# Attention with two experts per token: the second attention product with the probabilities as stationary operand

## The chip, the cores and the metric

The kernel runs on one core of one Trainium2 chip. The metric is the device time of one execution in microseconds (us). A core has five engines with a queue of instructions each: TensorE (PE; the loading of its stationary operand is shown apart, as PEld), VectorE (DVE), ScalarE (ACT), GpSimd (POOL) and SyncE (SP, which issues most DMAs). Each engine works through its queue in order and waits at semaphores for the others.

## The reference

```python
# attention: q, k, v are [4, 8, 768, 64]; each row sees 4 sink keys and the last 128 keys
scores = np.matmul(q, k.transpose(0, 1, 3, 2)) / np.sqrt(D)
scores = np.where(is_sink | in_window, scores, -1e9)
a = np.exp(scores - scores.max(-1, keepdims=True))
a = a / (a.sum(-1, keepdims=True) + 1e-9)
x = np.matmul(a, v)                                  # -> [3072 tokens, 512]
# experts: 8 of them, two for each token
noisy = x @ w_gate + np.log1p(np.exp(x @ w_noise)) * noise
top2 = the two largest of noisy; top2_w = softmax over these two
out[t] = sum over both: top2_w * (np.maximum(x[t] @ w1[e], 0) @ w2[e])
```

## The kernel before

The program is written as a list of operations with a planner. Each `op(engine, cost, priority, function, r=, w=, u=)` names its engine, a cost in us that the author gave it, a priority and what it reads and writes; `Plan.run` plays the list through and so fixes the order of the instructions on each engine. The priorities are place numbers plus the offsets of the table `PR`. `plan.rings` gives the number of buffers of each name; an operation on buffer n waits for all work on buffer n minus that number.

There are two phases. Phase one is the attention of four batches, each of four pairs of heads (`HP`), each pair in three steps (`NJ`) of 256 rows: 48 steps, called n below. One step holds four blocks u: two row blocks j of 128 rows times two heads h. Behind every fourth pair the routing of that batch is mixed in (logits, top two, where each token goes). Phase two has the logits and the routing of the last batch and then the experts, in which PE multiplies without a break. Expert 0 begins on tokens of the first three batches while the last batch is routed.

A step runs like this, with the names in the profile:

- `turn` (tile T, L283): PE transposes keys and queries of the step; ACT copies them to `kq`.
- `qk` (tile S, L310): the scores, as two matmuls that use 64 of PE's 128 rows each, side by side. ACT (`prev`, L313) and DVE (`cur`, L318/L320) put the window together in `cbuf`, 132 numbers for a row: four sink keys and 128 keys of the window.
- `mins` (L330): DVE takes the maximum of each row; POOL subtracts it (L197); ACT takes the exponential (L337).
- `sums` (L340) and `sums_i` (L348): DVE adds up each row of `cbuf` and takes the reciprocal, kept in `ri` for the whole batch.
- `ptr` (tile P, L368): PE transposes the four blocks of probabilities; ACT copies them to `CT`; `ptr_m` (CM, L378 on DVE or L380 on POOL) makes the copy with the part above the diagonal. The row of a key in the window is either in this block of keys or the one ahead, so the second product is `CT` times the values `vn` of the block ahead plus `CM` times the difference `dv` of the two blocks.
- `pv` (tile X, L394 and L397): the second product with the values as stationary operand, 64 columns wide, and the transposed probabilities moving, 128 columns. The heads of a pair go to the two halves of PE's columns and run side by side. The result is transposed: 64 dimensions by 128 rows.
- `pctr` (L385), `sink_c`, `sinks` (L406): the four sink keys, from a packed tile `pcbuf`, turned by PE, copied by ACT to `ps`, then two matmuls with `vr` (sink values) stationary.
- `pv_c` (L414): ACT copies the transposed result to `xtn`. `rows` (L419): PE transposes it back to rows; `rows_c` (L422): DVE multiplies by `ri`, and SP stores the rows (`xr`) to the table `x_rows` in HBM.
- `logits` (lines 605 to 645, twelve times: three per batch): `proj` (L616) multiplies the not yet normalised `xtn` with `wbd`, in which each head has its own columns, four matmuls side by side in four strips of 32 columns; ACT copies, PE turns (`turn`, L624), DVE scales each head by `ri` (L627) and adds the heads up (L632).

In the trace a float32 matmul has two records, since PE goes through its data twice, with a load of the stationary operand ahead of each; a float32r matmul and a transpose have one.

Of the kernel before, what the change touches and what calls it, by code (L numbers as in the profile page):

```python
# [9 lines left out]
F32 = mybir.dt.float32  # L10
# [7 lines left out]
OP = mybir.AluOpType  # L18
AX = mybir.AxisListType
BIG = 1.0e30  # L20
PR = dict(dv_pool=2, cm_pool=10, gap=3, pc_pool=0, warm=1, cur=-28.393, cur1=3.934, cur1_0=-210.795, cur1_9=-0.214,
          cur_0=-6.435, cur_9=42.546, dv=-181.673, dv_0=-58.475, dv_9=-165.981, exps=924.339, exps_0=-284.526,
          exps_9=-135.434, ga=442.815, gt=5.527, ksink=329.474, ksink_9=351.649, lg=5.452, load_qk=4.916, load_v=-10.311,
          mins=-1.124, mins_0=-130.078, mins_9=-231.976, nosink=115.551, nosink_0=201.297, nosink_9=23.605,
          pcopy=-1100.148, pcopy_0=54.064, pcopy_9=13.8, plow=6.687, plow_0=155.036, plow_9=-170.043, prev=-313.725,
          prev_0=560.262, prev_9=8.445, ptr=-158.634, ptr_0=-7.014, ptr_9=481.977, ptr_c=113.881, ptr_c_0=180.788,
          ptr_c_9=110.108, ptr_m=-225.012, ptr_m_0=-135.409, ptr_m_9=-137.504, pv=-1.694, pv_0=1.459, pv_9=2.578,
          pv_c=-36.493, pv_c_0=-19.005, pv_c_9=0.119, qk=-419.785, qk_0=3.807, qk_9=316.006, rows=-857.853,
          rows_0=-458.314, rows_9=34.438, rows_c=-1553.261, rows_c_0=-208.37, rows_c_9=-15.709, rt=-558.501, sink_c=2.596,
          sink_c_0=-90.91, sink_c_9=-279.362, sinks=-714.907, sinks_0=-12.828, sinks_9=261.99, sub=318.235, sub_0=521.605,  # L30
          sub_9=182.999, sums=78.667, sums_0=135.936, sums_9=-1.546, sums_i=-160.405, sums_i_0=280.185, sums_i_9=-301.562,
          t0=11.199, t2=-37.957, tgroup=71.501, tgroup_0=-63.73, tgroup_9=-56.402, tgroup_c=-1595.788, tgroup_c_0=7.035,
          tgroup_c_9=-3.093, w1=579.923, ksink_0=-652.007, stay=3844.16, pctr_0=71.802, sinkv=185.095, sc_dve=2,
          pctr=-325.901, pctr_9=-655.681)
# [165 lines left out]
def attention(tc, plan, consts, cst, sh, q, k, v, xbuf):  # L200
# [4 lines left out]
    KW = 128 + NS  # L205
    NP = sh.B * HP
    plan.rings.update(vr=2, kn=2, qn=2, vn=2, dv=2, skn=2, sqn=2, kq=2, C=5, mn=3, sm=4, ri=2, pc=3,
                      CT=2, CM=2, ps=3, xr=3, S=2, P=1, T=1, X=2, xtn=5, lt=1, lm=1, lg=2)
# [8 lines left out]
    m1 = consts.tile([128, NS], F32, name="m1")  # L217
    nc.vector.tensor_copy(m1, m0[:, :NS])
    nc.vector.memset(m0[:, :NS], 0.0)

    cbuf = consts.tile([128, plan.rings["C"], 4, KW + 1], F32, name="cbuf")
    nc.gpsimd.memset(cbuf[:, :, :, KW:], 1e-9)

    pcbuf = consts.tile([128, plan.rings["pc"], 128], F32R, name="pcbuf")
    nc.gpsimd.memset(pcbuf.bitcast(F32), 0.0)
    bit = [consts.tile([128, 1], dt, name=nm) for nm, dt in (("biti", I32), ("bit", F32))]
# [6 lines left out]
    def C(n):  # L233
        return cbuf[:, n % plan.rings["C"], :, :KW]
# [18 lines left out]
    def sink_hi(b):  # L253
        nc.scalar.activation(get("vr", b, [128, 2, HP, 2, D], F32R), vs(b), AF.Copy)

    def sink_lo(b):

        t = get("vr", b)
        nc.vector.scalar_tensor_tensor(t, t.bitcast(F32), bit, vs(b), op0=OP.mult, op1=OP.add)
# [10 lines left out]
    def load_v(g):  # L270
        nc.sync.dma_start(get("vn", g, [128, 2, NB, D]),
                          dram(v, g * 2 * S * D, [[D, 128], [S * D, 2], [128 * D, NB], [1, D]]))

    def dv(g, eng):
        x = get("vn", g)
# [49 lines left out]
    def cur1(n):  # L325
        c = C(n)[:, 2:, NS:2 * NS]
        nc.vector.tensor_tensor(c, c, m1[:, None, :].to_broadcast([128, 2, NS]), op=OP.add)
# [10 lines left out]

    def sums(n):
# [1049 lines left out]
```

## Time and profile before

| | before |
|---|---|
| median of 3 runs | 805.64 us (805.34 to 808.08) |
| profiled execution, from the first to the last instruction (span) | 802.8 us |
| left around the span, against the median | 2.8 us |
| PE busy | 772.3 us, 96% |
| DVE busy | 434.3 us, 54% |
| POOL busy | 441.5 us, 55% |
| ACT busy | 342.6 us, 43% |
| mean granted PE clock | 0.993 |

No time of the profiled execution other than its span is given, so the 2.8 us beside it are the median less the span. Busy time on PE counts a matmul from its start to its modelled end, and matmuls overlap: a new one may start every 0.11 us while each is counted as 0.27 us. So a busy PE is read from how closely the starts follow each other, and the share of busy time only says that there are few breaks. In the rows of the trace "128*64 128x128" says that the stationary operand is 128 rows by 64 columns and that the result is 128x128 in size as the program counts it (128 moving columns for L394), and xN is the count of records.

### The profile page before, as it was taken

How to read it: one execution, taken by the hardware profiler on the slowest of the kernel's cores; microseconds unless marked ns; L12 is line 12 of the kernel's file. 1: busy time of each engine (PE TensorE's matmuls, PEld its weight loads, DVE VectorE, ACT ScalarE, POOL GpSimd, SP SyncE). 2: the span in 40 equal slices, each digit the busy share in tenths (PEclk: the TensorE clock that was granted, in tenths of full speed). 3: DMA queues.
4: the chain of work that ended last, by engine and by line, in shares of the span. 5: the costliest groups of instructions: out<-in, count | busy, mean ns of one | idle time of the engine just before them, and what ended most of it. 6: DMA issues, size and time to landing. Idle time of an engine off the chain costs nothing.

```text
span 802.8 us, 13806 instructions
## 1 busy us (share of the span) xinstructions
PE 772.3 (96%) x4753; PEld 656.1 (82%) x4753; DVE 434.3 (54%) x1115; ACT 342.6 (43%) x695; POOL 441.5 (55%) x669
## 2 busy tenths in 40 slices
PE   7999999899798999999999999999999999999996
PEld 4776777677577888988988898899889999999994
DVE  5888897798565345354435434542553363364320
ACT  5877778686420334244233413332442343334121
POOL 5757657778604447473745456374636647366222
PEclk9999999999999999999999999999999999999998
DMA  6769767845526196264526535561744365174133
GB/s 121 169 150 200 162 155 207 181 120 129 152 90 175 22 257 152 45 140 128 102 38 158 141 56 94 144 119 37 147 123 94 73 172 121 26 175 97 32 40 40
DMA packets 151193, 96.03 MB, mean 120 GB/s; under 512 B 100528, under 2 KB 129200, under 8 KB 151120
## 3 DMA queue, kind: packets, MB, share of 16 engines
q1 hardware_dynamic: 137744, 67.93, 32.6%
q0 software_dynamic: 13376, 27.19, 19.4%
q8 instruction: 38, 0.62, 0.3%
q14 instruction: 35, 0.29, 0.1%
HBM read 66.89 MB, written 28.20 MB: 118 GB/s over the span
## 4 chain that ended last, share of the span: by engine, by line
PE 64%; issue 4%; DMA 2%; POOL 2%; DVE 1%; SPq 0%; ACT 0%; POOLq 0%; DVEq 0%; ACTq 0%
PE H L1070 11%; PE H L1072 10%; PE H L1071 10%; PE Y L1099 10%; PE Y L1101 10%; PE Y L1100 10%; POOL out L1123 1%; PE Y L1104 1%; PE Y L1105 1%; DMA xg<-x_rows,idg 1%; DMA out<-y,idx 1%; DMA st<-in_moe_w 1%; SPq L1268 0%; PE T L947 0%; PE X L616 0%
## 5 line engine op out<-in xcount | busy, mean ns | idle before, releaser
L903 POOL DMA_INDIRECT xg<-x_rows,rt_idq x174 | 175.8, 1010 | 62.1 <-issue 51.7
L1070 PE MATMUL H<-skn,w 128*128 128x384 f32 (+4 forms) x512 | 178.3, 348 | 0.0
L1072 PE MATMUL H<-skn,w 128*128 128x384 f32 (+4 forms) x512 | 176.8, 345 | 0.0
L1071 PE MATMUL H<-sqn,w 128*128 128x384 f32 (+4 forms) x512 | 176.3, 344 | 0.0
L1088 DVE SCALAR_TENSOR_TENSOR h<-H,h 128x384 fp32r<-128x384 f32 (+4 forms) x168 | 75.5, 469 | 184.7 <-ACT h L1081 184.5
L1081 ACT ACTIVATE h<-H 128x384 fp32r<-128x384 f32 (+4 forms) x128 | 64.6, 505 | 249.4 <-PE H L1072 249.3
L1132 POOL COPY spacer<-h 1x1 f32<-1x1 f32 x88 | 26.6, 303 | 167.3 <-ACT h L1081 167.1
L1123 POOL DMA_INDIRECT out<-y,idx x53 | 89.2, 1683 | 50.4 <-ACT y L1108 34.6
L1070 PEld LDWEIGHTS H<-skn,w 128*128 128x128 f32 x512 | 96.6, 189 | 7.7 <-issue 0.8
L1071 PEld LDWEIGHTS H<-sqn,w 128*128 128x128 f32 x512 | 96.6, 189 | 6.9
L1072 PEld LDWEIGHTS H<-skn,w 128*128 128x128 f32 x512 | 96.4, 188 | 3.0
L1101 PE MATMUL Y<-w2b,h 128*128 128x512 f32 x192 | 75.2, 392 | 1.1 <-DVE h L1088 1.1
L1099 PE MATMUL Y<-w2b,h 128*128 128x512 f32 x192 | 75.5, 393 | 0.6 <-ACT h L1081 0.6
L1099 PE MATMUL Y<-w2a,h 128*128 128x512 f32 x192 | 75.5, 393 | 0.0
L1100 PE MATMUL Y<-w2b,h 128*128 128x512 f32 x192 | 75.2, 392 | 0.0
L1100 PE MATMUL Y<-w2a,h 128*128 128x512 f32 x192 | 75.1, 391 | 0.0
L1101 PE MATMUL Y<-w2a,h 128*128 128x512 f32 x192 | 74.9, 390 | 0.0
L197 POOL TENSOR_TENSOR cbuf<-cbuf,mn 128x528 f32<-128x528 f32 x48 | 52.6, 1098 | 18.5 <-DVE mn L330 10.7
L310 PE MATMUL S<-kq 64*128 64x264 f32 (+1 forms) x384 | 56.4, 410 | 1.0 <-DVE ri L348 0.5
L961 ACT ACTIVATE skn<-xtn 128x512 fp32r<-128x512 f32 (+2 forms) x46 | 27.9, 606 | 63.3 <-DVE xtn L952 63.2
L197 DVE TENSOR_TENSOR w<-st,w 128x1024 fp32r<-128x1024 f32 x28 | 34.3, 1224 | 17.8 <-ACT w L1008 17.8
L1101 PEld LDWEIGHTS Y<-w2b,h 128*128 128x128 f32 x192 | 36.1, 188 | 9.4 <-DVE h L1088 1.6
(209 smaller groups left out, 1359.6 us busy)
## 6 DMA issues: line engine op xcount, KB each, us to landing
st<-in_moe_w SPq DMA_DIRECT2D x36, 512.0 KB
st<-in_moe_w SPq DMA_DIRECT2D x112, 128.0 KB
out<-zt SPq DMA_DIRECT2D x31, 256.0 KB
vn<-in_v SPq DMA_DIRECT2D x16, 384.0 KB
x_rows<-xr SPq DMA_DIRECT2D x48, 128.0 KB
kn<-in_k SPq DMA_DIRECT2D x30, 192.0 KB
qn<-in_q SPq DMA_DIRECT2D x30, 192.0 KB
xg<-x_rows,rt_idq POOLq DMA_INDIRECT x174, 2.9
```

What stands on the lines that cost most here:

```text
L197: eng.tensor_tensor(out, a, b, op=OP.subtract)
L310: nc.tensor.matmul(p[:, :2 if j else 1], kq(g)[r, j // 2, 2 + j % 2, NS:], x[:, :2 if j else 1], start=True, stop=True)
L903: nc.gpsimd.indirect_dma_start(out=x[:, i, :], out_offset=None, in_=xbuf.rearrange("r (q d) -> (r q) d", d=sh.SW), in_offset=bass.Indirect ...
L1070: nc.tensor.matmul(p, w[:, 0, i], xh, start=(i == 0), stop=False)
L1071: nc.tensor.matmul(p, w[:, 0, i], xl, start=False, stop=False)
L1072: nc.tensor.matmul(p, w[:, 1, i], xh, start=False, stop=(i == DC - 1))
L1081: nc.scalar.activation(get("h", FC * q + f, [128, 2 * 128 * FIRST], F32R)[:, :width], get("H", FC * q + f), AF.Relu)
L1088: nc.vector.scalar_tensor_tensor(h[:, o:o + s1 - s0], p[:, s0:s1], 0.0, h[:, s0:s1].bitcast(F32), op0=OP.max, op1=OP.subtract)
L1099: nc.tensor.matmul(p, hh, w[:, 0], start=(f == 0), stop=False)
L1100: nc.tensor.matmul(p, hh, w[:, 1], start=False, stop=False)
L1101: nc.tensor.matmul(p, hl, w[:, 0], start=False, stop=(f == FC - 1))
L1123: d = nc.gpsimd.indirect_dma_start(out=out, out_offset=bass.IndirectOffsetOnAxis(ap=c["idx"][:size(e, t), e, t:t + 1], axis=0), in_=get("y ...
```

## The change

`pv` has its operands exchanged: the transposed probabilities `CT` and `CM` (128 by 128) are stationary, and the values move: 65 columns, of which the last one is all ones, so that the row sum comes out of the same product (64 for `dv`). The result stands in rows. Four blocks of 66 columns (`DV`) stand beside each other in tile X. The sinks are one matmul with `ps` stationary and 264 moving columns, with a column of ones for each block (`units`, `counts`) and 1e-9 added through row 64 of `pcbuf`. `sums` and `sums_i` go; `ri` is the reciprocal of the sum columns in PSUM, and `rows_c` normalises before the transposes. `rows` then transposes the normalised rows and ACT copies them to `xtn` (`rows_t`). The logits are taken from that: 128 tokens of `xtn` stationary, `wgn` (16 columns) moving, eight matmuls that add up in PSUM, and one copy. The two loads `wgn` replace four of `wbd`. `cur1` goes from DVE to POOL. The table `PR` is new: with `dv_pool` 0 all sixteen `dv` are on DVE, of which eight were on POOL, and with `cm_pool` 7 (was 10) of 12 twelve more `ptr_m` are on DVE.

```diff
+    DV = D + 2
-                      CT=2, CM=2, ps=3, xr=3, S=2, P=1, T=1, X=2, xtn=5, lt=1, lm=1, lg=2)
+                      CT=2, CM=2, ps=3, xr=3, S=2, P=1, T=1, X=2, xtn=5, lg=2)
...
+    vnbuf = consts.tile([128, plan.rings["vn"], 2, NB, DV], F32, name="vnbuf")
+    nc.gpsimd.memset(vnbuf[:, :, :, :, D:], 1.0)
+    vrbuf = consts.tile([128, plan.rings["vr"], 2, HP, 2, DV], F32R, name="vrbuf")
...
-        nc.vector.tensor_tensor(c, c, m1[:, None, :].to_broadcast([128, 2, NS]), op=OP.add)
+        nc.gpsimd.affine_select(c, c, pattern=[[0, 2], [-1, NS]], base=0, channel_multiplier=1, compare_op=OP.is_ge, fill=-BIG)
...
-    def sums(n):
-        nc.vector.tensor_reduce(get("sm", n, [128, 4]), cbuf[:, n % plan.rings["C"]], op=OP.add, axis=AX.X)
...
     def pv(n):
...
-                    nc.tensor.matmul(o, get("vn", g)[:, h, max(j - 1, 0), :], get("CT", n)[:, u, :], start=(u < 2),
-                                     stop=False, skip_group_check=True)
+                    nc.tensor.matmul(o[:, :D + 1], get("CT", n)[:, u, :], vn(g)[:, h, max(j - 1, 0), :D + 1], start=(u == 0),
+                                     stop=False, skip_group_check=True)
...
-                    nc.tensor.matmul(o, get("dv", g)[:, h, j - 1, :], get("CM", n)[:, u, :], start=False, stop=False,
+                    nc.tensor.matmul(o[:, :D], get("CM", n)[:, u, :], get("dv", g)[:, h, j - 1, :], start=False, stop=False,
...
-        for a in range(2):
-            nc.tensor.matmul(get("X", XA[n])[:, a, :], get("vr", b)[:, a, i].rearrange("p h d -> p (h d)"), get("ps", n),
-                             start=False, stop=True, skip_group_check=True)
+        nc.tensor.matmul(get("X", XA[n])[:, :4 * DV], get("ps", n), vr(b)[:, :, i].rearrange("p a h d -> p a (h d)"),
+                         start=False, stop=True, skip_group_check=True)
+
+    def ri(n):
+        nc.vector.reciprocal(get("ri", n, [128, 4]), out(n)[:, :, D])
+
+    def rows_c(n):
+        nc.vector.tensor_tensor(get("xr", n, [128, 4, D], F32, "tail"), out(n)[:, :, :D],
+                                get("ri", n)[:, :, None].to_broadcast([128, 4, D]), op=OP.mult)
+
     def rows(n):
...
+            nc.tensor.transpose(x[:, c * 128:(c + 1) * 128], get("xr", n)[:, 2 * c:2 * c + 2].rearrange("p h d -> p (h d)"), idf)
...
-            op("PE", .95 if jj else .7, n + .6 + P(g, "pv"), lambda n=n: pv(n),
-               r=[("vn", g), ("CT", n), ("dv", g), ("CM", n), ("X", xa)], w=[("X2", xa)], kind=2)
+            op("PE", .92 if jj else .7, n + .6 + P(g, "pv"), lambda n=n: pv(n),
+               r=[("vn", g), ("CT", n), ("dv", g), ("CM", n), ("X", xa)], w=[("X2", xa)])
...
     def proj():
-        p = get("X", xa, [128, 4, 128], F32, "ps")
-        for i, g in enumerate(pairs):
-            nc.tensor.matmul(p[32 * i:32 * (i + 1), :2, :], c["wbd"][:, i].rearrange("p h a e -> p (h a e)"),
-                             get("xtn", g)[:, jj * 256:(jj + 1) * 256], start=True, stop=True)
+        p = get("X", xa, [128, 512], F32, "ps")
+        for t in range(2):
+            for i, g in enumerate(pairs):
+                nc.tensor.matmul(p[:, 2 * E * t:2 * E * (t + 1)], get("xtn", g)[:, (2 * jj + t) * 128:(2 * jj + t + 1) * 128],
+                                 c["wgn"][:, i].rearrange("p a e -> p (a e)"), start=(i == 0), stop=(i == HP - 1))
...
-    def turn():
-    def scale():
-    def total():
```

Where the first logits of the first batch stand, PE's queue had before (T: keys and queries turned, S: scores, P: probabilities turned, `lt`: the logits to be turned):

```order
L616 MATMUL X<-xtn,wbd 32x256 x4
L385 MATMUL X<-idf,pcbuf 128x128
L283 MATMUL T<-idf,kn 128x128 x2
L283 MATMUL T<-idf,qn 128x128 x2
L310 MATMUL S<-kq 128x264 x4
L394 MATMUL X<-CT,vn 64x128 x4
L397 MATMUL X<-CM,dv 64x128 x4
L406 MATMUL X<-ps,vr 128x128 x2
L310 MATMUL S<-kq 128x264 x4
L419 MATMUL X<-idf,xtn 128x128 x2
L368 MATMUL P<-idf,cbuf 128x128 x4
L624 MATMUL X<-idf,lt 128x128 x2
```

The same place in PE's queue has now:

```order
L406 MATMUL X<-vnbuf,CT 128x65 x4
L409 MATMUL X<-dv,CM 128x64 x4
L623 MATMUL X<-wgn,xtn 128x16 x8
L304 MATMUL T<-idf,kn 128x128 x2
L304 MATMUL T<-idf,qn 128x128 x2
L378 MATMUL P<-idf,cbuf 128x128 x4
L417 MATMUL X<-vrbuf,ps 128x264
L331 MATMUL S<-kq 128x132 x2
L331 MATMUL S<-kq 128x264 x2
L430 MATMUL X<-idf,xr 128x128 x2
```

The second product keeps its eight matmuls, now with 128 result rows and 65 or 64 moving columns; the logits go from four to eight matmuls and lose their transposes; the sinks go from two to one. The transposes of the rows (L430) stand behind the scores, and read `xr`, which DVE writes.

On DVE a stretch with the rows of two steps read before (mn: the maxima, sm: the sums, xr: the normalised rows):

```order
L340 TENSOR_REDUCE sm_722<-cbuf_146 128x4
L330 TENSOR_REDUCE mn_734<-cbuf_146 128x4
L348 RECIPROCAL ri_264<-sm_722 128x2x2
L320 COPY_PREDICATED cbuf_146<-le_137,S_736 128x2x128
L422 TENSOR_TENSOR xr_759<-X_637,ri_264 128x256
L422 TENSOR_TENSOR xr_767<-X_639,ri_264 128x256
L320 COPY_PREDICATED cbuf_146<-le_137,S_748 128x2x128
```

and a stretch of that kind reads now:

```order
L351 TENSOR_REDUCE mn_601<-cbuf_143 128x4
L421 RECIPROCAL ri_637<-X_575 128x4
L421 RECIPROCAL ri_639<-X_578 128x4
L424 TENSOR_TENSOR xr_642<-X_575,ri_637 128x256
L424 TENSOR_TENSOR xr_649<-X_578,ri_639 128x256
L341 COPY_PREDICATED cbuf_143<-le_136,S_634 128x2x128
L341 COPY_PREDICATED cbuf_143<-le_136,S_651 128x2x128
```

The reduction for the sums is gone, the reciprocals read tile X, so that they stand behind the sinks of PE, and PE's transposes of the rows stand behind `xr`, where before they stood behind ACT's copy and `xr` came last.

More of the change, by code (lines that the diff above doesn't have):

```diff
@@ L20 @@
 BIG = 1.0e30
[L21 to L34, printed above, removed]
@@ L205, in attention @@
     KW = 128 + NS
+    DV = D + 2
     NP = sh.B * HP
-    plan.rings.update(vr=2, kn=2, qn=2, vn=2, dv=2, skn=2, sqn=2, kq=2, C=5, mn=3, sm=4, ri=2, pc=3,
-                      CT=2, CM=2, ps=3, xr=3, S=2, P=1, T=1, X=2, xtn=5, lt=1, lm=1, lg=2)
+    plan.rings.update(vr=2, kn=2, qn=2, vn=2, dv=2, skn=2, sqn=2, kq=2, C=5, mn=3, ri=3, pc=3,
+                      CT=2, CM=2, ps=3, xr=3, S=2, P=1, T=1, X=2, xtn=5, lg=2)
     get, op = plan.get, plan.op
@@ L233, in C, with vn, vr, counts @@
     def C(n):
-        return cbuf[:, n % plan.rings["C"], :, :KW]
+        return cbuf[:, n % plan.rings["C"]]
+    def vn(g):
+        return vnbuf[:, g % plan.rings["vn"]]
+    def vr(b):
+        return vrbuf[:, b % plan.rings["vr"]]
+    def counts():
+        for r in range(plan.rings["vr"]):
+            for a in range(2):
+                nc.vector.tensor_copy(vrbuf[:, r, a, :, :, D:], units[:, None, 2 * a:2 * a + 2, :].to_broadcast([128, HP, 2, 2]))
     def vs(b):
@@ L381, in ptr_m, with out @@
                                     compare_op=OP.is_ge, fill=0.0)
+    def out(n):
+        return get("X", XA[n])[:, :4 * DV].rearrange("p (u d) -> p u d", d=DV)
     def pctr(n):
-        x = get("X", XA[n], [128, 4, 128], F32, "ps")
-        nc.tensor.transpose(x[:, 2, :], pcbuf[:, n % plan.rings["pc"], :].bitcast(F32), idf)
+        x = get("X", XA[n], [128, 512], F32, "ps")
+        nc.tensor.transpose(x[:, 4 * DV:4 * DV + 128], pcbuf[:, n % plan.rings["pc"], :].bitcast(F32), idf)
     def pv(n):
-        x = get("X", XA[n])
         for m in range(2):
@@ L535, in routing_setup @@
     c = cst
-    wbd = c["wbd"] = tmp.tile([128, HP, 2, 2, E], F32, name="wbd")
-    nc.gpsimd.memset(wbd, 0.0)
+    c["wgn"] = tmp.tile([128, HP, 2, E], F32, name="wgn")
     exact = dict(allow_small_or_imprecise_dtypes=True)
@@ L584, in gate_loads, with load @@
 def gate_loads(nc, plan, cst, sh, w_gate, w_noise, noise):
[L585 to L589 removed]
+    c = cst
+    E, HP, T = sh.E, sh.H // 2, sh.T
+    def load(i):
+        nc.sync.dma_start(c["wgn"][:, :, i, :], dram((w_gate, w_noise)[i], 0, [[E, 128], [128 * E, HP], [1, E]]))
     def noises():
@@ L594, in gates @@
     def gates():
-        for x in range(4):
-            plan.dma(6 + x, lambda x=x: load(x // 2, x % 2), .4, r=[("xrow", 4 + x)], w=[("gw", x)], n=1.3)
+        for x in range(2):
+            plan.dma(6 + x, lambda x=x: load(x), .8, r=[("xrow", 4 + 2 * x)], w=[("gw", x)], n=1.3)
         plan.dma(10, noises, 1.5, r=[("xrow", 8)], w=[("nzs", 0)], n=1.3)
@@ L1357, in moe_kernel @@
             plan.run()
-            live = {kx: t for kx, t in plan.live.items() if kx[0] in ("st", "w1", "w2a", "xtn", "ri", "xg", "skn", "sqn")}
+            live = {kx: t for kx, t in plan.live.items() if kx[0] in ("st", "w1", "w2a", "xtn", "xg", "skn", "sqn")}
         sb = both.enter_context(tc.tile_pool(name="msb", bufs=1))
         ps = both.enter_context(tc.tile_pool(name="mps", bufs=1, space=bass.MemoryType.PSUM))
-        p2 = Plan(nc, {"sb": sb, "ps": ps, **pools}, {kx: plan.rings[kx] for kx in ("st", "xtn", "ri", "xg")})
+        p2 = Plan(nc, {"sb": sb, "ps": ps, **pools}, {kx: plan.rings[kx] for kx in ("st", "xtn", "xg")})
         p2.live.update(live)
```

103 lines of the change are left out of this document (46 added, 57 removed).

## The prediction

> **What bounds the kernel now.** I read the page first, then the stretches between the stage boundaries, then PE's own instructions in order of time, since PE's busy share cannot say how tight they stand.
>
> ```profile
> PE 772.3 (96%) x4753; PEld 656.1 (82%) x4753; DVE 434.3 (54%) x1115; ACT 342.6 (43%) x695; POOL 441.5 (55%) x669
> ```
>
> The columns of the next rows are start and end, length, and the busy us of each engine with its instructions, then PE's granted clock, DMA share and GB/s.
>
> ```profile
> 23.00:198.00 175.00, 168.60 (x1665) 127.16 (x1665) 150.90 (x414) 133.32 (x352) 122.29 (x237) 1.00 0.70 163
> 198.00:219.50 21.50, 15.05 (x142) 11.65 (x141) 13.42 (x34) 9.68 (x23) 13.27 (x17) 0.92 0.54 153
> 219.50:258.00 38.50, 35.65 (x213) 27.49 (x214) 22.98 (x86) 7.23 (x14) 10.20 (x19) 1.00 0.44 124
> 258.00:303.00 45.00, 43.32 (x219) 36.96 (x217) 18.78 (x47) 16.51 (x26) 18.01 (x25) 0.96 0.54 141
> 303.00:766.00 463.00, 462.92 (x2286) 416.40 (x2287) 210.43 (x494) 157.31 (x244) 255.81 (x329) 1.00 0.47 105
> ```
>
> The attention lasts until about 219.5. In its steady part (23 to 198) PE pauses 175.0 - 168.6 = 6.4 us, DVE is second with 150.9. From 303 to 766 the experts hold PE without a gap and are not touched. So what PE gains or loses ahead of 219.5 moves the end almost one for one. The next rows are PE in order of time (start, length, xN records).
>
> ```profile
> 62.70 0.64 PE L616 MATMUL X<-xtn,wbd 128*32 128x256 f32 x8
> 63.27 0.33 PE L385 MATMUL X<-idf,pcbuf 128*128 128x128 f32 x1
> 63.44 0.38 PE L283 MATMUL T<-idf,kn 128*128 128x128 f32 x2
> 63.66 0.38 PE L283 MATMUL T<-idf,qn 128*128 128x128 f32 x2
> 63.97 1.16 PE L310 MATMUL S<-kq 64*128 64x264 f32 x8
> 65.06 0.66 PE L394 MATMUL X<-CT,vn 128*64 128x128 f32 x8
> 65.55 0.61 PE L397 MATMUL X<-CM,dv 128*64 128x128 f32 x8
> 66.08 0.44 PE L406 MATMUL X<-ps,vr 128*128 128x128 f32 x2
> 66.45 1.16 PE L310 MATMUL S<-kq 64*128 64x264 f32 x8
> 67.55 0.44 PE L419 MATMUL X<-idf,xtn 128*128 128x128 f32 x2
> ```
>
> Each row begins where the one ahead has handed over: this is a queue at its limit. Transposes follow at 0.11 us (63.44 to 63.66, two of them). From the two at 63.66 to the scores at 63.97 are 0.31, so 0.09 more: the price of going from the whole array to a part of it. The second product has 16 records in 1.02 us (65.06 to 66.08): two heads side by side, so eight places of 0.11, plus a first load and a change at the end. The sinks take 0.37 up to the scores, 0.28 without the change.
>
> **The price of the new product.** A float32 matmul loads its stationary operand for each of its two passes. With 64 columns and two heads sharing the time, and 128 moving columns, that load stood behind the moving data. Now 128 columns are loaded for 65 moving ones. The trace has one place of just this kind, late in the routing, a float32 stationary of 128 by 128 with 49 moving columns (the second row gives the shortest, median and longest record in ns):
>
> ```profile
> 253.77 0.94 PE L859 MATMUL X<-rt_idr,y 128*128 128x49 f32 x7
> L859 PE MATMUL X<-rt_idr,y x8: 204/275/275, 253.7 to 254.4; 128*128 128x49 f32 x8
> ```
>
> Seven records span 0.94 us, the last takes 0.275: (0.94 - 0.275) / 6 = 0.111 us from start to start. 49 columns moved are under half of 128, yet a pass is no shorter than one with 128; what sets the pace is the load. The other row is the load for transposes:
>
> ```profile
> 61.90 0.20 PEld L419 LDWEIGHTS X<-idf,xtn 128*128 128x128 f32 x2 [0.39 <-ACT xtn L414]
> L419 PEld LDWEIGHTS X<-idf,xtn 128*128 128x128 f32 x96 | 10.2, 142 | 12.0 <-ACT xtn L414 6.6 <-issue 2.2 <-ACT cbuf L337 0.7
> ```
>
> Two loads in 0.20, one of 0.142: they follow at 0.06. So a pass of the new product costs between 0.06 and 0.111. I take 0.111, from the row that is a product and not a transpose.
>
> The Trainium skill speaks of this too. On the page "TensorE: Matmul & The Clock Gate", section "Back-to-back issue gap", it gives about 81 ns per matmul as the sustained pace of pairs of load and matmul at 128 moving columns. The L859 row does not agree with it for float32 operands; by 81 ns the sum below would end near no change, which is the third rival.
>
> **The change part by part.** Counts are from the groups of the attention:
>
> ```profile
> L394 PE MATMUL X<-CT,vn 128*64 128x128 f32 x384 | 31.4, 284 | 1.8 <-ACT ps L401 1.7
> L397 PE MATMUL X<-CM,dv 128*64 128x128 f32 x320 | 26.1, 276 | 0.0
> L616 PE MATMUL X<-xtn,wbd 128*32 128x256 f32 x72 | 5.8, 391 | 0.2 <-DVE lm L627 0.2
> L624 PE MATMUL X<-idf,lt 128*128 128x128 f32 x18 | 3.4, 272 | 0.0
> ```
>
> The chain of waits gives the pace of a float32r matmul of 512 columns (H, start and length):
>
> ```profile
> 220.60 0.23 PE H L1071
> 220.83 0.23 PE H L1072
> ```
>
> The 704 records of L394 and L397 are 32 steps of 16 and 16 steps of 12 (a first row block has no CM).
>
> 1. Product and sinks. Before: 0.09 for the change ahead, 1.02, 0.28, together 1.39 us; with 12 records two places less, 1.17. Now: 16 x 0.111 = 1.78, or 12 x 0.111 = 1.33. The one sink matmul has 264 columns; by those 0.23 for 512 they take 0.12; with its load uncovered 0.23; I take 0.17. Together 1.95 and 1.50. More: 32 x 0.56 + 16 x 0.33 = 23.2 us. Nothing covers it.
> 2. Logits. Before 0.57 (62.70 to 63.27) and two transposes of 0.11: 0.79. Now eight matmuls of two passes with 16 columns: 16 x 0.111 = 1.78. More: 0.99 each, nine times in the attention 8.9 us, three times in phase two 3.0 us.
> 3. Transposes of rows: two per step as before, no cost.
>
> PE in the attention: +32.1 us.
>
> 4. DVE, POOL, ACT:
>
> ```profile
> L340 DVE TENSOR_REDUCE sm<-cbuf 128x4 f32<-128x532 f32 x48 | 33.6, 699 | 10.0 <-ACT cbuf L337 9.7
> L327 DVE TENSOR_TENSOR cbuf<-cbuf,m 128x8 f32<-128x8 f32 x16 | 5.7, 357 | 0.1
> L632 DVE TENSOR_REDUCE lg<-lm 128x32 f32<-128x256 f32 x9 | 5.3, 589 | 0.1
> L627 DVE TENSOR_TENSOR lm<-X,ri 128x256 f32<-128x256 f32 x9 | 3.7, 410 | 0.2 <-PE X L624 0.2
> L197 DVE TENSOR_TENSOR dv<-vn 128x640 f32<-128x640 f32 x8 | 7.4, 928 | 0.0
> L378 DVE TENSOR_TENSOR CM<-P,ge 128x512 f32<-128x512 f32 x8 | 5.5, 689 | 4.1 <-ACT CT L371 4.1
> L422 DVE TENSOR_TENSOR xr<-X,ri 128x256 f32<-128x256 f32 x48 | 19.4, 418 | 8.3 <-ACT xtn L414 2.9 <-PE X L419 2.7 <-ACT cbuf L313 1.6
> L348 DVE RECIPROCAL ri<-sm 128x4 f32<-128x4 f32 x48 | 8.2, 170 | 0.4
> ```
>
> DVE loses 33.6 + 5.7 + 5.3 + 3.7 = 48.3 us and gains eight `dv` (7.4) and twelve `ptr_m` (12 x 0.689 = 8.3): 32.6 us less, from an engine that does not set the pace: worth nothing by itself. POOL loses those twenty and gains `cur1`; ACT has the same copies; both stay under PE. The set-up adds a few memsets and selects on POOL and four copies on DVE, each no longer than the 0.689 of a full CM; they lie under the first loads, 0, at worst 2 us. SP issues two gate loads for four and the rows' stores earlier: nothing waits there.
>
> 5. Waits. The rows' transposes used to wait for one copy on ACT; now they wait for a reciprocal and a product on DVE, 0.17 + 0.42 = 0.59 us, and tile X, of which there are two, is held until ACT's copy after them. If all of that lay open it would be 48 x 0.59 = 28 us; nothing would be the other end. In the order there stand scores or transposes of 0.4 to 1.1 us between sinks and rows, and DVE has more room. I let these waits replace the 6.4 us of PE's present pauses: net 0.
> 6. The end of the attention and the start of the experts:
>
> ```profile
> 219.53 0.64 PE L616 MATMUL X<-xtn,wbd 128*32 128x256 f32 x8 [1.26 <-DVE sqn L197]
> 257.46 0.66 PE L947 MATMUL TX<-idf,xg 128*128 128x128 f32 x4 [2.75 <-DMA xg<-x_rows,idg]
> 258.90 0.63 PE L1070 MATMUL H<-skn,w 128*128 128x512 f32 x1
> 259.33 0.63 PE L1071 MATMUL H<-sqn,w 128*128 128x512 f32 x1
> ```
>
> From 198 to 219.5 PE pauses 21.5 - 15.05 = 6.45 us, 1.26 of it ahead of the last batch's logits, behind DVE; its products are longer now and DVE freer, so I take 4 of these as gone (between 0 and 6.45). At 257.46 it waits 2.75 us for the gather of the last batch and then runs at half speed (0.43 from H to H in place of 0.23; a clock of 0.96 over 45 us is 1.8 us). The logits bring 3.0 us more work into that gap, and the chain to the gather loses L627, L632 and two transposes: both go, -2.75 and -1.8.
>
> Sum: 802.8 + 32.1 + 3.0 - 4 - 2.75 - 1.8 = 829.4 us span; with the 2.8 us between span and median 832 us.
>
> **The rivals.**
> - Loads as fast as for transposes. At 0.06 the steps cost 0.96 + 0.17 and 0.72 + 0.17 in place of 1.39 and 1.17: 32 x 0.26 + 16 x 0.28 = 12.8 us less; logits 0.96 against 0.79, 12 x 0.17 = 2.0 more. With the 8.5 us of point 6: 805.6 - 12.8 + 2.0 - 8.5 = 786 us, faster. For it speaks the row of L419, and the cost of 0.92 in the plan, which is 16 x 0.0575. Against it the L859 row, the only product of this form. It decides where a pass falls under about 0.08. Chance 0.09.
> - DVE in the way. If of the 0.59 us of point 5 two thirds lie open in each step, 48 x 0.4 = 19 us come on top: 851 us. For it: an order laid out with 0.92 for a product that takes 1.78. Against it: DVE's 32.6 us less. Chance 0.11.
> - A pass near 0.08, midway between the two rows, with the load partly under the moving data. Steps 1.30 + 0.17 and 0.97 + 0.17, so 32 x 0.08 - 16 x 0.03 = 2 us more, logits 12 x 0.51 = 6 more, less 8.5: 805 us, no change. Nothing in the trace has this pace for float32. Chance 0.04.
>
> **How the numbers follow.** The forecast has the remaining 0.76. Its own range: with all of PE's pauses gone (6.4 and 2.45 more, 1.7 of clock at 0.92 over 21.5 us) and the sinks at 0.12 it is 819; with 2 us of set-up, none of the 8.5 us of point 6 gained, and 0.1 us of open waits per step 847. The range of 8 in 10 reaches a little beyond, to 815 and 850, and leaves out the first and third rival and the far half of the second. A difference of 0.5%, 4 us, is about what a measurement of this kernel can tell from none. Faster by more: the first rival and a part of the third, 0.10; within: 0.03; slower: the forecast and the second, 0.87.
>
> **What would show it.** Starts of L406 and L409 at 0.11 us, and about 1.8 us from the first to the end for 16 records, prove point 1; 0.06 there proves the first rival. L623 with 16 records should take 1.8 us. The first H of the experts should stand near 248 rather than 220, with PE still without long pauses. Waits of PE on `xr`, or of L398 on X, of more than 10 us together would mean the second rival. Wrong would be the forecast if PE's pauses in the attention were larger than they look, so that the new passes fit into them.

## The result, and the profile after

The changed kernel takes 838.58 us (median of 4 runs, 833.90 to 839.05), the kernel before on the same chip 805.49 us (803.11 to 808.08): 1.0398 times as long, 95% interval 1.0365 to 1.0431. Forecast were 832 us. The profiled execution has a span of 836.6 us. Where the runs of one kernel lie more than 1.5% apart, as in two of the experiments, only the faster ones are compared. The page of the profiled execution, answering to the first row of the prediction:

```profile
span 836.6 us, 13779 instructions
PE 811.5 (97%) x4777; PEld 712.2 (85%) x4777; DVE 407.7 (49%) x1050; ACT 339.4 (41%) x695; POOL 432.3 (52%) x670
PEclk9999997999999999999999999999999999999999
```

PE has 24 matmul records more than before but 39 us more of busy time, PEld 56 us; DVE has 26.6 us less. The third row has one digit below 9: the mean clock, 0.983, hides stretches at a lower one, to which I come back.

The stretches between the stages (columns as in the prediction):

```profile
23.00:198.00 175.00, 172.41 (x1403) 148.57 (x1402) 108.22 (x287) 110.64 (x297) 90.37 (x188) 0.95 0.65 150
198.00:252.00 54.00, 48.58 (x409) 41.30 (x409) 34.11 (x106) 30.57 (x80) 34.41 (x61) 1.00 0.42 112
252.00:290.00 38.00, 35.38 (x200) 29.40 (x200) 20.42 (x81) 6.88 (x14) 9.24 (x15) 0.91 0.43 134
336.00:798.00 462.00, 461.00 (x2277) 414.73 (x2278) 210.62 (x495) 157.14 (x244) 257.30 (x328) 1.00 0.46 105
```

In the same 175 us PE starts 1403 records where it started 1665, and PEld has 148.57 us of loads where it had 127.16: fewer matmuls fit, because each needs a longer load. PE is fuller than before (172.41 against 168.60). The stage of the experts (336 to 798) is as long as before. The lost time lies ahead of it.

PE in order of time (start, length, xN records); the last two rows are the end of the attention:

```profile
222.45 1.00 PE L406 MATMUL X<-vnbuf,CT 128*128 128x65 f32 x8
223.29 1.06 PE L409 MATMUL X<-dv,CM 128*128 128x64 f32 x8
224.19 0.28 PE L430 MATMUL X<-idf,xr 128*128 128x128 f32 x1
...
250.31 1.93 PE L623 MATMUL X<-wgn,xtn 128*128 128x16 f32 x16 [0.77 <-DVE sqn L197]
252.09 0.53 PE L1061 MATMUL H<-skn,w 128*128 128x512 f32 x1
...
286.38 1.04 PE L938 MATMUL TX<-idf,xg 128*128 128x128 f32 x4 [2.62 <-DMA xg<-x_rows,idg]
```

The 16 records of one step's product take 224.19 - 222.45 = 1.74 us, and the 16 of the logits 252.09 - 250.31 = 1.78, though they move 65 or 64 and 16 columns. The first H of the experts stands at 252.1 instead of 220.1. At 286.38 PE still waits 2.62 us for the gather of the last batch.

What PE waits for up to 255 us (us in total, times, longest):

```profile
PE P L378 <- ACT CT L381: 2.2, 4, 0.6
PE X L430 <- DVE xr L424: 1.3, 2, 1.0
```

The new wait of the rows' transposes on DVE (`xr`) comes to 1.3 us in 48 steps.

The trace's record of the granted clock has only two values here, full and half. The stretches at half, start and length in us, leaving out the tail after the last matmul of the experts:

```
before   210.5 3.4                                                  258.3 3.4
after    71.5 3.4   129.5 3.4   136.3 6.8   194.3 3.4               252.4 3.4   286.5 3.4
```

Ahead of the experts that is 3.4 us before and 17.1 (rounded sum of five windows of 3.41) after. A stretch of x us at half clock costs x/2 where PE has work all the time.

### The profile page after: what moved, and what is told of

Read it like the earlier page. It is cut to its first block, busy times and chain, and to the rows that moved or that the text cites. A ratio compares the mean times of both kernels' runs of the same rounds, so it can differ in the third digit from the quotient of the medians.

```text
span 836.6 us, 13779 instructions
## 1 busy us (share of the span) xinstructions
PE 811.5 (97%) x4777; PEld 712.2 (85%) x4777; DVE 407.7 (49%) x1050; ACT 339.4 (41%) x695; POOL 432.3 (52%) x670
## 4 chain that ended last, share of the span: by engine, by line
PE 87%; issue 4%; ACT 3%; DMA 2%; POOL 2%; DVE 1%; SPq 1%; POOLq 0%; ACTq 0%; DVEq 0%
PE H L1061 10%; PE H L1063 10%; PE H L1062 10%; PE Y L1090 9%; PE Y L1092 9%; PE Y L1091 9%; PE S L331 6%; PE X L406 5%; PE X L409 4%; PE X L623 3%; PE P L378 3%; PE T L304 3%; POOL out L1114 1%; PE X L430 1%; PE X L417 1%
## 5 line engine op out<-in xcount | busy, mean ns | idle before, releaser
L894 POOL DMA_INDIRECT xg<-x_rows,rt_idq x174 | 177.7, 1021 | 61.6 <-issue 51.7
L197 POOL TENSOR_TENSOR cbuf<-cbuf,mn 128x528 f32<-128x528 f32 x48 | 54.8, 1142 | 25.1 <-DVE mn L351 16.2
L406 PE MATMUL X<-vnbuf,CT 128*128 128x65 f32 x384 | 49.0, 271 | 0.6 <-ACT CT L381 0.3
L406 PEld LDWEIGHTS X<-vnbuf,CT 128*128 128x128 f32 x384 | 47.1, 193 | 2.0 <-ACT ps L413 1.1
```

The lines of the kernel that those rows point to most:

```text
L406: nc.tensor.matmul(o[:, :D + 1], get("CT", n)[:, u, :], vn(g)[:, h, max(j - 1, 0), :D + 1], start=(u == 0), stop=False, skip_group_check=True)
L894: nc.gpsimd.indirect_dma_start(out=x[:, i, :], out_offset=None, in_=xbuf.rearrange("r (q d) -> (r q) d", d=sh.SW), in_offset=bass.Indirect ...
```

## The experiments

A kernel's runs differ mostly by their clock. The product of a run's time and its mean granted clock is about the time at full clock, so below it parts what a kernel does from what the clock adds. Between runs of one kernel it varies by 0.1 to 0.3% in most of the rows, by 0.5 to 0.6% in e6 and b1 and by 0.75% in before. It also takes off half of the stretch at half clock behind the last matmul, which slows no matmul: 1.2 to 2.8 us in these traces, so differences under 1.5 us are not read. All times in us; the ratio is to the kernel before on the same chip.

| | median | ratio (95%) | clock of the runs | time x clock, mean | first H |
|---|---|---|---|---|---|
| before (27 runs beside the experiments) | 803.8 to 804.5 | 1 | 0.987 to 0.997 | 798.3 | 220.1 |
| after | 838.58 | 1.0398 (1.0365, 1.0431) | 0.983 to 0.989 | 825.0 | 252.1 |
| e3: values 96 wide | 837.15 | 1.0400 (1.0378, 1.0422) | 0.985 to 0.988 | 825.3 | 250.9 |
| e1: logits 128 wide | 831.67 | 1.0334 (1.0315, 1.0352) | 0.992 to 0.995 | 826.7 | 245.7 |
| e7: both wide | 832.10 | 1.0352 (1.0312, 1.0392) | 0.990 to 0.998 | 826.8 | 245.9 |
| e6: one pass | 820.75 | 1.0208 (1.0163, 1.0253) | 0.957 to 0.971 | 789.8 | 235.6 |
| e2: planner told the costs (two runs) | 867.17 | none | 0.970 to 0.973 | 842.4 | 282.5 |
| e4: sums back | 837.46 | 1.0391 (1.0358, 1.0425) | 0.989 to 0.995 | 828.9 | 252.1 |
| e12: e1 and sums back | 836.05 | 1.0422 (1.0379, 1.0465) | 0.986 to 0.996 | 829.7 | 249.2 |
| e5: logits in strips (one run) | 864.42 | none | 0.969 | 837.6 | 276.2 |
| e8: gather later | 831.08 | 1.0346 (1.0320, 1.0371) | 0.988 to 0.992 | 822.8 | 247.1 |
| e11: e1 and gather later | 826.65 | 1.0287 (1.0263, 1.0310) | 0.995 to 0.998 | 823.6 | 245.3 |
| b1: before, gather later | 799.07 | 0.9949 (0.9929, 0.9969) | 0.991 to 0.997 | 794.8 | 220.2 |
| e9: one pass, wide, gather later | 811.82 | 1.0101 (1.0081, 1.0122) | 0.979 to 0.983 | 796.4 | 227.9 |

The other runs took 879 and 880 (e2) and 880 to 883 (e5, whose trace is of one of these). One or two runs give no interval.

**Is it the load that sets the pace? More moved columns (e3).** The values of the `CT` matmuls (L407) move as 96 columns per pass, with no operation more and the same order of instructions; those of `CM` (L410) still move 64.

```diff
+    DX = 96
...
-                    nc.tensor.matmul(o[:, :D + 1], get("CT", n)[:, u, :], vn(g)[:, h, max(j - 1, 0), :D + 1], start=(u == 0),
+                    nc.tensor.matmul(o, get("CT", n)[:, u, :], vn(g)[:, h, max(j - 1, 0), :], start=(u == 0),
```

> The changed kernel with 96 moving columns in each pass of the second product in place of 65 and 64 (blocks of 96 columns in tile X, the added columns are never read). Theory (the load sets the pace): a step's 16 records still follow at 0.11 us, 1.78 us for a step; time the same or, if the fuller passes keep the clock up, up to 6 us less than 838.6. Rival (moved columns set the pace): 16 passes x 31 columns x 0.85 ns = 0.42 us more in a step, 18 us more in all, 857.

The expectation speaks of every pass, but the edit widens only 8 of a step's 16 records, so the rival's price is about half of its 18 us, some 847. Measured 837.15 against 838.58, with intervals that overlap almost wholly, and a time at full clock of 825.3 against 825.0. In PE's order of time of e3:

```profile
222.97 1.03 PE L407 MATMUL X<-vnbuf,CT 128*128 128x96 f32 x8
223.84 0.58 PE L410 MATMUL X<-dv,CM 128*128 128x64 f32 x4
```

Eight records of 96 columns take 0.87 us, 0.109 each; the eight of 65 columns took 0.84. Half as many columns again cost nothing: they stand behind the load. The Trainium skill, page "TensorE: Matmul & The Clock Gate", section "LDWEIGHTS (loading the stationary operand)", says that the time of a load goes by the stationary operand's columns; an estimate by its formula is 107 ns for 128 of them, and the 109 and 111 ns here agree. The pace of 81 ns in its section "Back-to-back issue gap", near the prediction's third rival, is not that of the float32 products here with 128 columns stationary, which take 0.105 to 0.115 us from start to start.

**The same for the logits (e1).** The moving operand is `wgn` repeated eight times, 128 columns instead of 16; the copy reads the first 16 of them.

```diff
-                nc.tensor.matmul(p[:, 2 * E * t:2 * E * (t + 1)], get("xtn", g)[:, (2 * jj + t) * 128:(2 * jj + t + 1) * 128],
-                                 c["wgn"][:, i].rearrange("p a e -> p (a e)"), start=(i == 0), stop=(i == HP - 1))
+                nc.tensor.matmul(p[:, 128 * t:128 * (t + 1)].rearrange("p (r x) -> p r x", x=2 * E),
+                                 get("xtn", g)[:, (2 * jj + t) * 128:(2 * jj + t + 1) * 128],
+                                 c["wgn"][:, i].rearrange("p a e -> p (a e)")[:, None, :].to_broadcast([128, 8, 2 * E]),
+                                 start=(i == 0), stop=(i == HP - 1))
```

> The changed kernel with one edit: the 16 columns that move in each logits matmul (L623) are moved eight times over, 128 columns, into columns of tile X that nobody reads. Theory (the load of the 128x128 float32 stationary sets the pace of a pass, and passes that mostly load count as a resting PE for the clock, so that the half-speed stretches at 71, 129, 136 and 194 us follow the logits): a group of 16 records still takes 1.7 to 1.9 us, the half-speed stretches of the attention get fewer (17 us of them now) and the time falls from 838.6 by 4 to 8 us. Rival (the clock falls for another cause, such as pauses): the groups take the same, the half-speed stretches stay, 838 within 2 us. If moved columns set the pace, a group would go from 1.8 to above 2.5 us and the time rise by 8 or more.

Eight times the data made the kernel faster, 831.67: 7 us by the medians, 5 by the ratios to before on the same chip, whose intervals do not touch. The same place in PE's order of time, first of after, then of e1:

```profile
69.13 1.91 PE L623 MATMUL X<-wgn,xtn 128*128 128x16 f32 x16
70.89 0.42 PE L304 MATMUL T<-idf,kn 128*128 128x128 f32 x2
71.15 0.38 PE L304 MATMUL T<-idf,qn 128*128 128x128 f32 x2
71.36 0.95 PE L378 MATMUL P<-idf,cbuf 128*128 128x128 f32 x4
71.97 0.57 PE L417 MATMUL X<-vrbuf,ps 128*128 128x264 f32 x1
72.46 1.69 PE L331 MATMUL S<-kq 64*128 64x132 f32 x8
```

```profile
69.16 2.00 PE L623 MATMUL X<-wgn,xtn 128*128 128x128 f32 x16
71.00 0.38 PE L304 MATMUL T<-idf,kn 128*128 128x128 f32 x2
71.22 0.38 PE L304 MATMUL T<-idf,qn 128*128 128x128 f32 x2
71.43 0.60 PE L378 MATMUL P<-idf,cbuf 128*128 128x128 f32 x4
71.79 0.36 PE L417 MATMUL X<-vrbuf,ps 128*128 128x264 f32 x1
72.08 0.94 PE L331 MATMUL S<-kq 64*128 64x132 f32 x8
```

The logits take as long (1.76 and 1.84 us), so the load sets the pace here too. But in after the scores behind them take 1.69 us in place of 0.94, and no row has a wait. It is the clock, as the stretches with such places show, of after and then of e1 (the clock is the fraction ahead of the last two columns):

```profile
63.00:76.00 13.00, 13.00 (x98) 11.18 (x98) 6.95 (x15) 8.33 (x22) 6.24 (x13) 0.87 0.54 133
120.00:143.20 23.20, 23.20 (x160) 20.62 (x160) 9.75 (x22) 11.48 (x32) 8.14 (x18) 0.78 0.54 129
```

```profile
63.00:76.00 13.00, 13.00 (x111) 11.29 (x109) 7.70 (x18) 8.98 (x24) 7.43 (x15) 1.00 0.59 134
120.00:143.20 23.20, 23.20 (x200) 20.79 (x200) 13.02 (x50) 14.43 (x41) 9.72 (x23) 1.00 0.51 130
```

PE is busy for all of 13.00 and 23.20 us in both kernels, yet only after runs at 0.87 and 0.78 and gets through 160 records where e1 gets through 200. The order of the instructions is the same. So the logits are paid for twice: in loads, and in a clock that goes to half after a stretch of loads with little moved behind them (the last section counts how little). Over all runs the clock is 0.983 to 0.989 in after and 0.992 to 0.995 in e1, while the time at full clock is the same or a little longer (826.7).

The Trainium skill, same page, section "HAM oscillation — how this bites in real kernels", ties half clock to pauses of PE of more than about 3.4 us. The length comes back here, in stretches of 3.41 us and multiples of it; the pause does not: in the 3.41 us ahead of 71.5, 129.5, 136.3 and 194.3 PE is busy throughout.

**Both widened (e7).**

> The changed kernel with both products filled up: 128 moving columns in the logits and 96 in the four CT matmuls of a step, the added columns never read. Theory (loads set the pace, and how much moves between them decides the clock): no half-speed stretch in the attention outside its end, time as with the wide logits alone or up to 3 us less, 828 to 833. Rival (wide values are a burden of their own): above 835.

832.10, that is e1 again, also at full clock (826.8). Widening the values brings nothing on top of e1; widening the logits on top of e3 brings 4 to 5 us, though here the intervals of the ratios overlap a little.

**Half of the loads (e6).** `CT`, `CM`, `dv` and a copy of the values (on ACT) are rounded to float32r, which takes one pass and one load per matmul. This leaves out the lower part of the numbers.

```diff
+    def vq(g):
+        nc.scalar.activation(get("vq", g, [128, 2, NB, DV], F32R), vn(g), AF.Copy)
...
-        nc.scalar.activation(get("CT", n, [128, 4, 128]), get("P", n + NJ), AF.Copy)
+        nc.scalar.activation(get("CT", n, [128, 4, 128], F32R), get("P", n + NJ), AF.Copy)
```

> The changed kernel with the operands of the second product rounded to float32r (CT, CM, dv, and a rounded copy of the values made by ACT), so that each of its matmuls loads its stationary once and makes one pass in place of two. Left out is the lower part of these numbers. Theory (the loads of the second product are what the change costs, 704 of them at 0.111 us): 352 loads fewer, 39 us of PE gone; without new waits 838.6 - 39 = 800; some of it will come back as waits of PE for the other engines, so 800 to 815. Rival (the new product is not what costs the time): above 825.

The 352 matmuls lose a pass each: 352 x 0.111 = 39 us. At full clock the kernel is 825.0 - 789.8 = 35.2 us faster than after, and faster than before by 8.5: the second pass and its load cost more than the whole change. The clock ate much of it:

```profile
23.00:198.00 175.00, 168.33 (x1282) 138.37 (x1282) 124.83 (x336) 136.05 (x350) 104.60 (x219) 0.92 0.70 166
198.00:250.00 52.00, 47.21 (x262) 41.26 (x263) 27.00 (x86) 20.32 (x49) 17.47 (x31) 0.70 0.32 87
```

Ahead of the first H at 235.6 PE is at half clock for 54.6 us; the last stretch is 30.7 us in one piece (208.3 to 239.0), and PE is busy 47.21 of the 52 us from 198 to 250. Against the expectation of 800 to 815 the measured 820.75 is too slow by this. The long stretch is nine windows of 3.41 us; the last section counts what moved in them.

**Did the planner's old cost do harm? (e2).** The planner is told what the operations take.

```diff
-            op("PE", .92 if jj else .7, n + .6 + P(g, "pv"), lambda n=n: pv(n),
+            op("PE", 1.78 if jj else 1.34, n + .6 + P(g, "pv"), lambda n=n: pv(n),
...
-    op("PE", .8, z, proj, ...)
+    op("PE", 1.8, z, proj, ...)
```

> The changed kernel with the planner told what the operations take: 1.78 and 1.34 us for the second product in place of 0.92 and 0.7, 1.8 us for the logits in place of 0.8. Only the order on the engines changes. Theory (PE's own work is the limit, 32 us more of it): within 4 us of 838.6. Rival (the order laid out with 0.92 makes the loss): 8 us faster or more.

Both theories missed: 867.17, 28.6 us slower than after. What PE waits for up to 290 us, and the steady part:

```profile
PE P L378 <- ACT cbuf L358: 8.1, 11, 1.1
PE X L430 <- DVE xr L424: 6.2, 9, 1.2
PE P L378 <- ACT CT L381: 4.3, 5, 1.0
```

```profile
23.00:198.00 175.00, 160.64 (x1267) 136.44 (x1264) 96.29 (x269) 103.98 (x267) 81.39 (x171) 0.94 0.59 135
```

In the order that the planner makes of these costs PE pauses 14.4 us in the 175, in place of 2.6; up to 290 us it waits most for the exponentials (`cbuf`, L358), the normalised rows (`xr`) and ACT's copies of the turned probabilities (`CT`). At full clock the kernel is 842.4 - 825.0 = 17.4 us slower; the other 11 are clock. The table of priorities was laid out with the old costs. The run does not show that the order in after costs nothing; it shows that correct costs alone give a worse one.

**What is DVE's relief worth? (e4, e12).** The 48 reductions that the change removed (0.70 us each, 33.6 together) are put back, their result unused; in e12 on top of e1.

```diff
+    def sums(n):
+        nc.vector.tensor_reduce(get("sm", n, [128, 4]), C(n), op=OP.add, axis=AX.X)
...
+            op("DVE", .0, n + .8 + 78.667, lambda n=n: sums(n), r=[("C", n)], w=[("sm", n)])
```

> The changed kernel with the row sums of before put back on DVE (48 reductions of 0.70 us, 33.6 us; their result is not used). Theory (DVE does not set the pace, so taking the sums away gained nothing): 0 to 4 us slower than 838.6. Rival (DVE's relief paid back a large part of PE's extra work): 10 us slower or more.

> The kernel with the wide logits (831.7, its clock steady) and the row sums put back on DVE, their result not used. Theory (DVE's relief of 33.6 us is worth only what its work stands in PE's way): 3 to 6 us slower than 831.7, as the first look at sums put back gives when its half-speed stretches are taken off. Rival one (worth nothing): within 2 us. Rival two (worth most of itself): 10 us or more.

e4 alone looks like nothing, 837.46 against 838.58. But its clock was higher, 0.989 to 0.995, and at full clock it is 828.9 against 825.0: 3.9 us slower. e12 against e1, both with the wide logits, gives 829.7 against 826.7, 3.0 us, and 836.05 against 831.67 in the medians with intervals that do not overlap. So the relief was worth 3 to 4 us, not nothing. The planner also moves some of PE's operations when `sums` is in its list, even at a cost of .0 (from 114 us on the order is another), and these runs do not part that from DVE's work. The pair e4 and e12 also limits e1's gain: in this order PE has 6.8 us of half clock ahead of the first H where after has 17.1, and the wide logits, which take that to none in the trace of e12, bring nothing in the medians (1.0422 against 1.0391, with intervals that overlap).

**Is it the form of the logits? (e5).** The logits in four strips of 32 columns with `wgn` stationary, as before the change, added up by a matmul with a 0/1 matrix:

```diff
+        for i, g in enumerate(pairs):
+            nc.tensor.matmul(p[32 * i:32 * (i + 1), :256], c["wgn"][:, i].rearrange("p a e -> p (a e)"),
+                             get("xtn", g)[:, jj * 256:(jj + 1) * 256], start=True, stop=True)
...
+    op("PE", .57, z, proj, ..., kind=2)
+    op("ACT", .27, z, strips, r=[("X", xa)], w=[("lt", li)])
+    op("PE", .44, z, turn, r=[("lt", li)], w=[("X", xa)])
```

> The changed kernel with the logits as side-by-side strips again: 16 columns of weights (padded to 32) stationary in four strips, 256 tokens moving, and the copied strips then go through one product with a 0/1 matrix of 16 columns, which turns them and adds the pairs in one. The logits stay those of the normalised rows, and nothing goes to DVE. Theory (16 loads of 128 columns at 0.111 us are the price of the new logits, with the half-speed stretches behind them): PE takes 0.57 + 0.44 us in place of 1.8, twelve times, 9 us less, and the clock gives back some more: 822 to 830. Rival (the logits are hidden or not the cause of the slow clock): 836 or more.

864.42 at best: a miss, and no answer to its question. I gave `proj` `kind=2`; the planner takes up an operation of another kind than the one before it only when none of the same kind is ready, so the last batch's logits stood only at 321 to 326, behind the expert work meant to cover its routing. Nothing was left to do then:

```profile
326.00:357.00 31.00, 13.49 (x85) 11.80 (x86) 18.28 (x85) 5.29 (x13) 16.22 (x23) 0.50 0.42 95
```

PE is busy for 13.49 of 31 us, at half clock. The run measured this placing, not the price of the strips. The trace also has 65 us of half clock ahead of the first H.

**The gap for the last batch's gather (e8, e11, b1).** The planner is told that the gather of the last batch takes 8 us rather than 3, which puts the transposes of the gathered rows, `TX`, 24 expert matmuls further back in PE's queue. Ahead of that PE's order is the same.

```diff
-        plan.op("Pool", 1.25, z, go, r=[("idg", int(not first))], w=[("xg", n)], lat=3)
+        plan.op("Pool", 1.25, z, go, r=[("idg", int(not first))], w=[("xg", n)], lat=3 if first else 8)
```

> The changed kernel with the planner told that the gathers of the last batch land 8 us after their issue in place of 3; only the order of phase two changes, PE has 24 more expert matmuls of 0.23 us ahead of the transposes of the gathered rows. Theory (in the prediction's point 6 the 2.75 us gap and the slow clock behind it did not go because PE's queue has the transposes too early, not because work was missing): the gap of 2.9 us at 283.5 and the half-speed stretch at 286.5 go, 838.6 falls by 3 to 5 us. Rival (the gap is set by the chain to the gather, whatever stands ahead): same within 1.5 us.

> The changed kernel with the wide logits (128 moving columns) and the later landing time for the gathers together, nothing left out. Theory (two separate losses, clock and gap): 838.6 - 7 - 2 to 4, so 827 to 830. Rival (both gains were the same few half-speed stretches): 831 or more.

> The kernel before with the later landing time for the gathers of the last batch, nothing else; only the order of phase two changes. Theory (PE's queue has the transposes of the gathered rows too early): the pause of 2.75 us at 254.7 and the half-speed stretch at 258.3 (1.7 us) go, 3 to 5 us faster than before. Rival (the pause moves elsewhere): within 1.5 us of before.

Expected were 3 to 5 us each. The gap is gone; here 250 to 300 in e8 and 219.5 to 258 in b1, where the prediction's row has 35.65 us of PE:

```profile
250.00:300.00 50.00, 50.00 (x284) 41.61 (x284) 25.59 (x94) 9.53 (x21) 13.19 (x22) 1.00 0.29 90
```

```profile
219.50:258.00 38.50, 38.32 (x223) 29.75 (x224) 22.92 (x85) 7.22 (x14) 10.30 (x19) 1.00 0.42 122
258.00:303.00 45.00, 44.69 (x239) 39.10 (x238) 22.10 (x53) 19.16 (x31) 23.23 (x31) 1.00 0.65 171
```

e8 gains 7.5 us in the median (4 by the ratios), but its attention, whose instructions stand in the same order as in after, ran with less half clock in the profile (7.1 us against 17.1). At full clock the edit is worth 2.2 us in e8, 3.1 in e11 against e1, and 3.5 in b1. e11 is the fastest form of the change that computes everything, 826.65. b1 is faster than both kernels: 799.07, 0.9949 of before (0.9929 to 0.9969).

**Everything together (e9).** e6 with 96 and 128 wide operands, the later gather, and one value buffer in place of two (`vn=1`) to make room.

> The one-pass kernel (second product in float32r, its lower part left out) with 96 moving columns in the CT matmuls, 128 in the logits, the later landing time for the gathers, and one buffer for the raw values in place of two to make room. Theory (loads set PE's work, what moves between them sets the clock): the one-pass kernel had 54.6 us at half speed ahead of the experts; most of it goes, the experts begin near 210, and the time is 790 to 803, at or under the kernel before. Rival (one pass leaves too little moving whatever is added, the clock stays down): 810 or more.

811.82, a miss by 9 us on the slow side, and slower than before: the rival's 810 or more. Its reason holds in part. The clock is better than e6's (0.979 to 0.983) and takes 15.4 us (811.82 - 796.4) where it took 31.0, but at full clock the kernel is 6.6 us slower, 796.4 against 789.8:

```profile
23.00:198.00 175.00, 163.31 (x1345) 134.50 (x1344) 129.84 (x355) 142.04 (x362) 108.84 (x225) 1.00 0.69 163
198.00:250.00 52.00, 46.25 (x265) 40.20 (x266) 27.55 (x100) 17.42 (x40) 19.10 (x33) 0.77 0.39 102
```

PE pauses 11.7 of 175 us, e6 6.7. Whether the single buffer or the order that the planner laid around it does this was not tried apart. Even at 0.77 in its last part PE still drops to half clock, with the wide operands.

## Why the prediction was right, and where it was not

The time came out 6.6 us above the 832, inside the range. In spans it is 836.6 against 829.4. The prediction put the first H near 248; its own terms give 249.2, since one of the three logits of phase two stands ahead of the first H. It stood at 252.1 (+2.9), and from there to the end it took 584.5 instead of 580.2 (+4.3).

1. **Product and sinks: right.** 0.109 to 0.111 us per pass, 1.74 us for 16 against 1.78. e3 and e1 show that the moved columns do not set the pace, which leaves the load, and e6 what a second pass with its load costs: 35 us. That decides against the first rival (0.06, as in transposes) and the third (0.08). The 0.06 was never the pace of a stream: it is the distance of two loads of a pair, mostly behind a pause, while in the trace before the transposes of L283 and L368 start 0.109 us apart (median). Nor is 0.11 the price of any record: the bfloat16 products of L724, with 128 columns stationary and 56 moving, start 0.026 apart. The sinks' matmul takes 0.25 us to the next start, not 0.17.
2. **Logits: right in their length** (1.76 to 1.80 against 1.78), but they had a second price that the prediction didn't have: the clock behind them, e1.
3. **Rows' transposes: right**, there is nothing to see of them.
4. **DVE's 32.6 us "worth nothing by itself": wrong.** e4 and e12 lose 3 to 4 us at full clock with the sums put back, with the reservation made there about the order. DVE was busy 54% on the whole, but 150.9 of 175 us in the steady part, and 108.2 after the change: the stage, not the share of the span, should have set its worth. Up to the first H, PE pauses 16.0 us before, 11.6 after and 14.7 in e4, so the relief shows in shorter pauses. Point 6 had taken 4 us off for these, partly for a freer DVE, so the sum held much of this worth under another name.
5. **Waits: right against the second rival, and lucky in the sum.** There are 1.3 us on `xr` against that rival's 19. But PE's pauses in the 175 us fell from 6.4 to 2.6, where point 5 had no change, and from 198 to the first H only from 6.45 to 5.4, where point 6 took 4 off. Together they fell by about what the sum had, in the other place.
6. **End of the attention and start of the experts: the step that failed, in its second half.** I took the 2.75 us of waiting for the gather and the 1.8 us of clock behind it as gone. The trace after has 2.62 us at 286.38 and 3.4 us of half clock right behind. The reasoning looked at the work that the logits add in that gap, and at the shorter chain to the gather, but not at where the planner would put `TX`: it counts the gather with 3 us whatever it takes, and between the first logits of the last batch and `TX` PE had 72 H and 57 Y before, and 60 and 45 after. 24 expert matmuls of about 0.23 us are 5.5 us less cover. Put back by e8, the gap goes; b1 shows that it cost the kernel before about the same.

The term that was missing is the clock. By time x clock, after is 825.0 - 798.3 = 26.7 us slower than before at full clock; of the 33.1 us between the medians some 6 are left for the clock (about 1 us of that may lie between the chips, since before took 805.5 there and 803.8 to 804.5 beside the experiments).

The two traces give the same by parts. Up to the first H, 32.0 us later than before, I added up the times from each start of PE's to the next, without its pauses and with half-speed time counted half.

| up to the first H, us | foretold | measured |
|---|---|---|
| PE's work at full clock | +33.1 | +29.7 (200.1 to 229.8) |
| PE's pauses | -4 | -4.4 (16.0 to 11.6) |
| half clock | 0 | +6.8 (17.1 us in place of 3.4) |

In the work the product, the sinks and `pctr` together cost 26.2 us more (23.2 foretold) and the logits 9.5 (9.9); the other transposes and the scores, which had no term, took 6 us less, and why is open. Behind the first H the gap of 2.62 us stayed, and two stretches at half clock (252.4 and 286.5) cost 3.4 us where none was foretold; 1.7 us came back elsewhere, where is open. So the forecast is near because errors of 3 to 7 us with both signs stood against each other: 6.8 and 6.0 on the one side, 3.4 in the work and smaller ones on the other. That part of its nearness is luck.

## What to carry to other kernels

Price a float32 product by its loads: two passes of about 0.11 us each with 128 columns stationary, whether 16, 65, 96 or 128 columns move. Here turning the operands round nearly doubled the price (1.74 us for 1.02), because two stationaries of 64 columns used to run side by side. In stretches where PE mostly loads, look at the granted clock of that stretch, not at the waits: more moved columns are free up to 128 and may keep it up. A wait for an indirect DMA in an in-order queue goes when the plan is told how long the transfer really takes, which alone made the kernel before 0.5% faster.

## What the runs showed of the hardware that I had not expected

- Half clock without a pause. After 1.8 us of loads of 128 columns with 16 moved each, and transposes behind them, PE went to half for 3.41 us or a multiple, with every start following the one ahead. With 128 moved columns in those 192 records of 4777, the clock of e1 stayed at full until 204.8, and the kernel was 5 to 7 us faster. More columns in the 384 records of L406 (e3) did nothing for it.
- What moves in a window of 3.41 us goes with the clock. In each trace all stretches at half clock start on one grid of 3.41 us. I added up the columns that PE's records moved in each window of that grid, with a matmul on half of the array counted half (a few records are missing from a trace, so the counts are rough). In the twelve traces without e6 and e9, from 20 us to the last matmul, 34 windows at full clock moved up to 1,560 columns, and 32 of them were followed by half clock. Of 21 with 1,560 to 1,800 it was 3, and of 2,691 with more it was 3, each after a window in which PE paused for half of the time. Of these 38 falls 11 followed a window with PE busy throughout. In e6 and e9 the line is less sharp: 8 of their 12 falls came behind windows of 1,800 columns and more. A group of logits takes 1.8 us and moves 256 columns, and that brings a window under the line when the whole group lies in it; in e3 the windows ahead of 134.4 and 185.6 were still at 1,440 and 1,408. The windows are counted after the runs, and no run was made to test the line.
- The way back goes with the same count. In all fourteen traces 39 windows at half clock moved up to 1,552 columns, and each was followed by another at half; of 27 with up to 1,850, 18 ended the stretch, and of 34 with more, 32. The first eight windows of e6's stretch of 30.7 us moved 752 to 1,944, the ninth, with the first expert matmuls, 3,584. Fewer columns pass at half clock, so a stretch may hold itself; that is not shown.
- The number of such stretches differs between executions of the same instructions (17.1 us in after, 7.1 in e8 up to the first H), which moves a kernel by 0.5 to 1%. The product of time and mean clock was steady within 0.3% in after and e4 and told 4 us apart where the medians could not.
